# Splitting the accumulation step and shortening start-up in an attention and mixture-of-experts kernel on one core

## The chip, the cores and the metric

The kernel runs on one core of one Trainium2 chip. The metric is the device time of one launch in microseconds (us), lower is better; the time before is the median of three runs. The engines are TensorE (PE; its weight loads are listed as PEld), VectorE (DVE), ScalarE (ACT), GpSimd (POOL) and SyncE (SP, which here only issues DMAs). PSUM is the memory that TensorE writes; the others read it from there.

## The reference

Attention of 8 batches, 8 heads, 576 positions and 64 numbers a head, with a window of 32 positions and 8 global positions, whose result feeds a layer with 8 experts, of which each token takes the best one. In short:

```python
scores = scale * np.matmul(q, k.transpose(0, 1, 3, 2))
mask = np.abs(pos[:, None] - pos[None, :]) <= window
mask = mask | is_global[:, None] | is_global[None, :]
scores = np.where(mask, scores, -1000000000.0)
attn = softmax(scores)
attn_out = np.matmul(attn, v)
x = attn_out.transpose(0, 2, 1, 3).reshape(B * S, H * D)   # 4608 x 512
logits = x @ w_gate
expert_idx = np.argmax(logits, axis=1)
gate_w = softmax(logits)[np.arange(N), expert_idx]
for e in range(8):                       # 512 -> 1024 -> 512
    h = np.maximum(x[expert_idx == e] @ w1[e], 0.0)
    out[expert_idx == e] = gate_w * (h @ w2[e])
```

## The kernel before, in words

The order is written by hand: each engine has a queue in the order of the program, and an engine whose next instruction waits does nothing behind it. So the place of a line in the text is its place in the engine's queue.

**Start-up (to 28 us).** q, k and v of batch 0 are loaded (`load_qk` L158, `load_v` L163), q and k are cast to fp16 (`cast_qk` L289) and transposed on TensorE (`trans_qk` L293), masks are built, and twelve indirect DMAs on GpSimd (L264) gather the rows of the 8 global positions of all 8 batches from v, k and q. `trans_g` (L313) transposes the k and q rows, `load_vg` (L171) puts the v rows beside v.

**Attention (28 to 268.8 us), 8 batches of 6 slices t.** Loop L653 to L722. A slice: TensorE computes the scores of the next slice (`scores` L386: mask L392, products L405), ScalarE their exponentials (`exps` L410), TensorE the product with v of this slice (`pvs` L414, one PSUM buffer) and the sums (`zs` L428). Two accumulators, one half f each, collect the windows (`merge` L440): for half 0 ScalarE copies the new columns (L453) and VectorE adds the overlapping ones of half 1 (L458), then the same with the halves exchanged. Into slices 1 to 4 of all but the last batch go the transposes of the next batch's k and q (TensorE L300, L298; copied out of PSUM by ScalarE L305 for k, by VectorE L302 for q, the "q copy"). They share a PSUM pool of two buffers, `trp`, with everything below. The next batch's casts stand on GpSimd (L658).

The routing of the batch before (`class Tail`, L486) is spread over the same slices: `gate` L504, `logits` L518, `route1` L551 (arg-max), `ranks` L585 (place within the expert), `route2` L596 (slot), `rows` L539 (token rows transposed back into fp16), `scatter` L619 (six indirect DMAs on GpSimd, 128 token rows each). The weights of experts 0 and 1 are loaded in batches 1 to 4 in pieces of 512 KB (`wload` L633) and cast (`wcast` L640).

**Routing of the last batch (268.8 to 304 us).** L723 to L763: `sum_globals` and the memsets of eight row buffers (L725) on GpSimd, the routing of batch 7 and of the global rows (`tg`), the last scatters, then the first gathers of the experts' rows.

**Feed-forward stage (304 to 450 us).** Loop L935: for each expert eight h blocks of four matmuls (L943), each block through relu (L829, ScalarE and VectorE in turns), with a weight piece of an expert two ahead cast after every second block (`castp` L846) and its buffer loaded again (`fetch` L839). Then the four row tiles of the next expert are transposed (`xtrans` L809: four transposes, and a copy on VectorE L814), and four output blocks of eight matmuls follow (L969), scaled (L821, L823) and scattered. Blocks for overfull experts follow to 502 us and are not touched.

Of the kernel before, what the change touches and what calls it, by code (L numbers as in the profile page):

```python
# [22 lines left out]
NG = 8  # L23
# [20 lines left out]
def kernel(  # L44
# [42 lines left out]
    def short(*shape):  # L87
        n = 1
        for d_ in shape:
# [6 lines left out]
        r = stage[2 + a // 1024][:, a % 1024 : a % 1024 + n]  # L96
        return r.rearrange("p (a b) -> p a b", b=shape[1]) if len(shape) > 1 else r
# [64 lines left out]
    def load_v(b):  # L162
        d = vb[b % 2]  # L163
        for t in range(NT):
# [57 lines left out]
    nc.vector.scalar_tensor_tensor(out=p8s, in0=p8f, scalar=float(H * S), in1=rowb, op0=ALU.mult, op1=ALU.add)  # L222
    hofff = short(H)
# [17 lines left out]
    nc.vector.tensor_reduce(out=gip, in_=pmf, op=ALU.add, axis=AX.X)  # L241
    ridx = ap_.tile([128, H], I32, name="ridx")
# [70 lines left out]
    def trans_g():  # L313
        for src, dst in ((kg, kgt), (qg, qgt)):
# [4 lines left out]
            nc.vector.tensor_copy(dst, ps[:, 0:256].rearrange("p (c n) -> p c n", c=4))  # L319
# [21 lines left out]
    trans_g()  # L341
    fill_kg(0, nc.vector)
# [97 lines left out]
    def merge(t, parts):  # L440
# [11 lines left out]
        for i in range(len(parts)):  # L452
# [33 lines left out]
    class Tail:  # L486
# [64 lines left out]
        def route1(self):  # L551
# [12 lines left out]
            self.ex = small("ex", [6, 8])  # L564
            nc.scalar.activation(out=self.ex[p, 0:J], in_=d[p, 0:J], func=AF.Exp)
# [30 lines left out]
        def route2(self):  # L596
# [19 lines left out]
            nc.scalar.activation(out=self.x16[p, 0:J, DM:ROW].bitcast(I32)[:, :, 0],  # L616
                                 in_=tokg if self.glob else tokt[:, b, :], func=AF.Copy)
# [32 lines left out]
    routing_constants()  # L650
    tail = done = None
    staged = []
    for b in range(B):  # L653
# [8 lines left out]
        if b:  # L662
            sum_globals(b - 1)
# [418 lines left out]
```

## Time and profile before

| | |
|---|---|
| median of 3 runs | 504.03 us (503.88 to 504.34) |
| the profiled execution | 504.14 us, of which the profile's span is 502.4 us |
| mean granted TensorE clock | 0.93 |
| busy: PE, DVE, ACT, POOL | 76%, 49%, 40%, 49% |
| DMA traffic | 84.45 MB |

The span is the stretch that the profile covers, from its first to its last instruction; the rest of the execution's own time (1.74 us) lies around it. A busy share is an average over stages with different limits, so each stage is read by its own rows: an answer in order of time gives what an instruction waited for in brackets, with the idle time before it; "issue" there means that the profile shows nothing that it waited for.

### The profile page before, as it was taken

The numbers are of one execution on the slowest core, as the hardware profiler recorded it, in microseconds if no ns is written. First come the engines' busy times: TensorE is split into PE (matmuls) and PEld (weight loads), VectorE is DVE, ScalarE is ACT, GpSimd is POOL, SyncE is SP. The second block draws the span as 40 slices with busy tenths as digits, with TensorE's granted clock in tenths as the row PEclk, the third lists the DMA queues.
The fourth block names the chain that finished last, engine by engine and source line by source line (L and its number), as shares of the span: only waits on it lengthen the run. The fifth ranks groups of instructions, "written<-read, shape, count | busy, mean of one in ns | idle before, by whom it ended". The sixth has DMA issues, their size and how long they took to land. (4 is left out here: it accounts for less than half of the span.)

```text
span 502.4 us, 16112 instructions
## 1 busy us (share of the span) xinstructions
PE 383.6 (76%) x6595; PEld 233.1 (46%) x6595; DVE 248.3 (49%) x696; ACT 199.6 (40%) x359; POOL 246.5 (49%) x391
## 2 busy tenths in 40 slices
PE   1478686878877888889886509868888688999991
PEld 0256454556655665656563304434444243444540
DVE  3433253646665456666676704684455253233330
ACT  2235353654755547555440003325244233223330
POOL 6732350660836608475437765346466564334441
PEclk9999797989999799999998656999999989999996
DMA  7979989695897957721010274888999862112011
GB/s 166 190 177 170 214 189 274 144 283 139 195 284 155 274 132 179 165 35 51 8 46 14 74 253 139 284 311 264 341 332 327 310 190 102 66 64 71 31 42 38
DMA packets 76270, 84.45 MB, mean 168 GB/s; under 512 B 45084, under 2 KB 58412, under 8 KB 76192
## 3 DMA queue, kind: packets, MB, share of 16 engines
q1 hardware_dynamic: 66896, 63.61, 48.4%
q0 software_dynamic: 9024, 19.37, 11.6%
q8 instruction: 54, 0.88, 0.8%
q10 hardware_dynamic: 272, 0.39, 0.3%
q14 instruction: 24, 0.20, 0.1%
HBM read 68.89 MB, written 16.16 MB: 169 GB/s over the span
## 5 line engine op out<-in xcount | busy, mean ns | idle before, releaser
L943 PE MATMUL h<-xts,wall 128*128 128x512 f16 x256 | 62.0, 399 | 10.4 <-ACT ht L833 9.8
L423 PE MATMUL pv<-wall 56*64 56x128 f32 x1536 | 61.2, 294 | 6.5 <-issue 5.4
L458 DVE TENSOR_TENSOR xt<-xt,pv 128x288 f32<-128x288 f32 x80 | 36.3, 454 | 59.4 <-ACT xt L453 58.9
L412 ACT ACTIVATE wall<-sc 128x1024 f32<-128x1024 f32 x48 | 49.1, 1024 | 34.1 <-PE sc L405 32.5
L453 ACT ACTIVATE xt<-pv 128x224 f32<-128x224 f32 x96 | 34.3, 358 | 61.9 <-PE pv L423 29.9
L969 PE MATMUL yp<-wall,ht 128*128 128x512 f16 x256 | 56.6, 379 | 0.0
L423 PEld LDWEIGHTS pv<-wall 56*64 56x64 f32 x1536 | 47.0, 143 | 17.1 <-issue 13.3
L471 POOL TENSOR_TENSOR xt<-xt 128x144 f32<-128x144 f32 x14 | 7.1, 508 | 93.6 <-DVE xt L458 93.6
L287 POOL CAST wall<-wall 96x768 f16<-96x768 f32 (+1 forms) x56 | 43.9, 824 | 9.3 <-DMA wall<-in_k_dram 8.4
L943 PEld LDWEIGHTS <-wall 128*128 128x128 f16 x256 | 25.9, 102 | 45.1 <-issue 18.4
L824 POOL DMA_INDIRECT out_dram<-y,xr x24 | 25.0, 1041 | 41.4 <-DVE y L823 26.7
L831 DVE TENSOR_SCALAR ht<-h 128x512 f16<-128x512 f32 x32 | 22.1, 690 | 45.6 <-PE h L943 45.6
L435 PE MATMUL z<-wall,onesel 56*32 56x128 f32 x1536 | 36.7, 295 | 4.6 <-issue 4.6
L545 PE MATMUL tr_x<-id,xt 128*108 128x128 f32 x192 | 33.7, 303 | 6.9 <-DVE sv L602 2.2
L969 PEld LDWEIGHTS <-ht 128*128 128x128 f16 x256 | 24.7, 98 | 28.3
L833 ACT ACTIVATE ht<-h 128x512 f16<-128x512 f32 x32 | 19.0, 596 | 37.9 <-PE h L943 37.9
L405 PEld LDWEIGHTS <-kt 64*64 64x64 f16 x1536 | 25.1, 111 | 14.8 <-issue 10.1
L821 ACT ACTIVATE y<-yp,xr 128x512 f32<-128x512 f32 x12 | 8.2, 687 | 57.5 <-PE yp L969 37.1
L300 PE MATMUL tr_qk<-idh,wall 96*128 96x96 f16 x192 | 14.9, 219 | 19.7 <-ACT wall L285 11.0
L622 POOL DMA_INDIRECT xslot_scr<-wall,si x25 | 24.9, 995 | 8.7 <-issue 5.1
L785 POOL DMA_INDIRECT xr<-xslot_scr,idx x24 | 25.5, 1062 | 7.0 <-POOL xr L784 6.7
L622 POOL DMA_INDIRECT xslot_scr<-x16x,si x24 | 23.9, 994 | 9.0 <-issue 4.3
(243 smaller groups left out, 703.7 us busy)
## 6 DMA issues: line engine op xcount, KB each, us to landing
st<-in_moe_w_dram SPq DMA_DIRECT2D x48, 512.0 KB
wall<-in_k_dram SPq DMA_DIRECT2D x32, 288.0 KB
wall<-in_q_dram SPq DMA_DIRECT2D x32, 288.0 KB
wall<-in_v_dram SPq DMA_DIRECT2D x96, 96.0 KB
wall<-in_moe_w_dram SPq DMA_DIRECT2D x16, 512.0 KB
wall<-vg SPq DMA_DIRECT2D x16, 96.0 KB
xslot_scr<-wall,si POOLq DMA_INDIRECT x25, 2.6
wall<-in_q_dram ACTq DMA_DIRECT2D x1, 384.0 KB
```

Source lines behind the costliest of these rows:

```text
L287: eng.tensor_copy(o, i_)
L405: nc.tensor.matmul(out=o[:, NG:WE].rearrange("p (r a) -> p r a", r=R) if part == 0 else o[:, 0:NG], lhsT=kt[b % 2][rr, c, sl, :], rhs=rhs, ...
L412: nc.scalar.activation(out=e.rearrange("p r c w -> p r (c w)"), in_=sc[:, :, 0 : 4 * WE], func=AF.Exp, scale=0.125)
L423: nc.tensor.matmul(out=pv[64 * r : 64 * r + 64, f, c * WE : (c + 1) * WE], lhsT=vt[ff, t, 64 * h : 64 * h + 64], rhs=e[ff, r, c, :], start ...
L435: nc.tensor.matmul(out=z[32 * c : 32 * c + 32, f, 0:WE], lhsT=onesel[ff, r, :], rhs=e[ff, r, c, :], start=(r == 0), stop=(r == 1))
L453: nc.scalar.activation(out=new[i][0], in_=new[i][1], func=AF.Copy)
L458: nc.vector.tensor_tensor(out=d_, in0=d_, in1=s_, op=ALU.add)
L545: nc.tensor.transpose(out=ps[p, 128 * c : 128 * c + 128], in_=src, identity=id32)
L622: d_ = nc.gpsimd.indirect_dma_start(out=xslot, out_offset=IndirectOffsetOnAxis(ap=self.si[p, j : j + 1], axis=0), in_=self.x16[p, j, :].bi ...
L785: d_ = nc.gpsimd.indirect_dma_start(out=xr.bitcast(I16), out_offset=None, in_=xslot, in_offset=IndirectOffsetOnAxis(ap=ix, axis=0), bounds ...
L943: nc.tensor.matmul(out=ps, lhsT=w1v[:, e, c, 128 * fb : 128 * fb + 128], rhs=xts[:, c, :], start=(c == 0), stop=(c == 3))
L969: nc.tensor.matmul(out=ps, lhsT=ht[:, fc, 128 * j : 128 * j + 128], rhs=w2v[:, e, fc, :], start=(fc == 0), stop=(fc == 7))
```

## The change

It has five parts. In the words of the new code:

1. **Start-up.** Five small gathers (global rows of batch 0 only) stand before the scores, with a small `trans_g0`; the twelve large ones move behind `routing_constants`, and `trans_g`, with `load_vg(1)`, moves into slice 3 of batch 0. Only slice 0 of v is loaded ahead of them. 
2. **Batch 0.** The casts of batch 1 move from GpSimd to VectorE, one pair at the head of each slice 2 to 5, and the transposes of batch 1 from slices 1 to 4 to slices 2 to 5.
3. **The two halves.** `merge` returns a function for one half; the q transposes and the q copy (or `gate(0)`) stand between `mx(0)` and `mx(1)`.
4. **Routing.** `route2` moves ahead of the product of slice 5; its weights (`weights`), the exponentials and token numbers (`exps`) become steps of their own; `rows(2, 0)` moves from the next batch to the end of slice 5; the eight memsets move to the head of batch 7; after the loop the last scatters of batch 6 stand ahead of `sum_globals(7)`.
5. **Weights and feed-forward.** A weight piece is two DMAs of 128x512 instead of one; the rows of w1 in a DMA are 2 KB long instead of 4 KB. The four transposes of the next expert's rows stand one behind each second h block instead of all behind the last.

```diff
 def load_v(b, t0=None):
-    for t in range(NT):
+    for t in range(NT) if t0 is None else (t0,):
 load_qk(0)
+load_v(0, 0)
-load_v(0)
-for dst, src in ((vgr, v), (kg, k), (qg, q)):
-    for i in range(4):
-        ...
-for s_ in range(2):
-    nc.sync.dma_start(out=vg..., in_=vgr...)
+gather_g(vg0, v, ridx0[0:64, 2:3])
+for dst, src in ((kg0, k), (qg0, q)):
+    for r in range(2):
+        gather_g(dst[:, 64 * r : 64 * r + 64], src, ridx0[0:32, r : r + 1])
+for h in range(H):
+    nc.sync.dma_start(out=vg[0:8, h, :], in_=vg0[8 * h : 8 * h + 8])
 load_vg(0)
+for t in range(1, NT):
+    load_v(0, t)
...
+def trans_g0():
+    for i, src in enumerate((kg0, qg0)):
+        ps = trp.tile([128, 512], FP32, tag="tr", name="tr_g0")
+        nc.tensor.transpose(out=ps[:, 0:32], in_=src, identity=id32[0:32, 0:32])
+        p4 = ps[:, 0:32].rearrange("p (c o g) -> p c o g", c=4, o=1)
+        if i:
+            nc.vector.tensor_copy(qgt[:, :, 0:8], p4[:, :, 0])
+        else:
+            nc.vector.tensor_copy(kt[0][:, :, :, HW : HW + NG], p4.to_broadcast([128, 4, NSL, NG]))
 load_qk(1)
-trans_g()
-fill_kg(0, nc.vector)
+trans_g0()
...
 def merge(t, parts):
-    for i in range(len(parts)):
+    def part(i):
         nc.scalar.activation(out=new[i][0], in_=new[i][1], func=AF.Copy)
         ...
+    return part
...
 def wload(e, w, i, st):
-    if w == 0:
-        nc.sync.dma_start(out=st, in_=moe_w1[e, 128 * i : 128 * i + 128])
-    else:
-        ...
+    for hf in range(2):
+        src = (moe_w1[e, 128 * i : 128 * i + 128, 512 * hf : 512 * hf + 512] if w == 0
+               else moe_w2[e, 256 * i + 128 * hf : 256 * i + 128 * hf + 128])
+        nc.sync.dma_start(out=st[:, 512 * hf : 512 * hf + 512], in_=src)
...
 routing_constants()
+for dst, src in ((kg, k), (qg, q), (vgr, v)):
+    for i in range(4):
+        h = 4 * (i // 2) + i % 2
+        gather_g(dst[:, i, :], src, ridx[:, h : h + 1])
 for b in range(B):
-        for pair in range(4):
+        for pair in range(4) if b else ():
             cast_qk(pair, nc.gpsimd, nc.gpsimd)
...
     if b:
         sum_globals(b - 1)
+    if b + 1 == B:
+        for x_ in xr01:
+            nc.gpsimd.memset(x_, 0.0)
     for t in range(NT):
         tr = t - 1 if b + 1 < B and 1 <= t <= 4 else None
+        if b == 0:
+            tr = t - 2 if t >= 2 else None
+            if tr is not None:
+                cast_qk(tr, nc.vector, nc.vector)
         if tr is not None:
             trans_qk(b + 1, tr, "k")
+            if b == 0 and t == 5:
+                trans_qk(b + 1, tr, "q")
+                load_qk(2)
         elif t == 0 and done is not None:
-            done.rows(2, 0)
+            done.rows(2, 1)
+            done.scatter()
...
             elif t == 5:
                 tail.rows(1, 1)
+                tail.route2()
         pv = pvs(b, t)
-        merge_x(b, t, pv)
+        mx = merge_x(b, t, pv)
+        mx(0)
         if tr is not None:
-            trans_qk(b + 1, tr, "q")
+            if not (b == 0 and t == 5):
+                trans_qk(b + 1, tr, "q")
         elif t == 0 and tail is not None:
             tail.gate(0)
+        mx(1)
...
             elif t == 4:
                 tail.rows(1, 0)
+                tail.exps()
             else:
-                tail.route2()
+                tail.rows(2, 0)
+                tail.weights()
+        elif t == 3:
+            trans_g()
+            ...
+            load_vg(1)
+            fill_kg(1, nc.gpsimd)
+done.rows(2, 1)
+done.scatter()
 sum_globals(B - 1)
-for x_ in xr01:
-    nc.gpsimd.memset(x_, 0.0)
 tail.gate(0)
-done.rows(2, 0)
 tail.gate(1)
 tail.logits(0)
-done.rows(2, 1)
-done.scatter()
...
         if fb % 2:
             castp(nc.scalar if fb % 4 == 1 else nc.vector)
+            if e + 1 < E:
+                j = fb // 2
+                xtrans(rows_of[e + 1][j], xtn[:, :, 128 * j : 128 * j + 128])
     if e + 1 < E:
-        xts = fp2.tile([128, 4, 512], FP16, tag="xts", name="xts")
-        for j in range(4):
-            xtrans(rows_of[e + 1][j], xts[:, :, 128 * j : 128 * j + 128])
+        xts = xtn
```

How the instructions stand now is shown at three places. The first is VectorE's queue in a slice of batch 1 with transposes (`xt` and `zt` are the accumulators, `pv` and `z` the products in PSUM, `tr_qk` the transposes; the last three are `logits` of batch 0). Before:

```order
L458 TENSOR_TENSOR xt_76<-xt_76,pv 128x4x6x12 x2
L302 COPY qt_81<-tr_qk 128x6x96
L458 TENSOR_TENSOR zt_78<-zt_78,z 128x2x6x12
L529 RECIPROCAL rz<-tr_lt 108x16
L532 TENSOR_TENSOR tmp<-tr_lt,rz 108x128
L536 TENSOR_REDUCE lg<-tmp 108x16
```

and in the changed kernel, there as from batch 1 on:

```order
L479 TENSOR_TENSOR xt_76<-xt_76,pv 128x4x6x12
L310 COPY qt_81<-tr_qk 128x6x96
L479 TENSOR_TENSOR xt_76<-xt_76,pv 128x4x6x12
L479 TENSOR_TENSOR zt_78<-zt_78,z 128x2x6x12
L552 RECIPROCAL rz<-tr_lt 108x16
L555 TENSOR_TENSOR tmp<-tr_lt,rz 108x128
L559 TENSOR_REDUCE lg<-tmp 108x16
```

The q copy stands behind one add instead of two. The second place is VectorE's queue in batch 0, slices 2 and 3, of the changed kernel (`wall` are the buffers of k and q):

```order
L295 CAST wall<-wall 96x2x6x64
L295 CAST wall<-wall 128x2x6x64
L479 TENSOR_TENSOR xt_75<-xt_75,pv 128x4x6x12
L310 COPY qt_82<-tr_qk 128x6x96
L479 TENSOR_TENSOR xt_75<-xt_75,pv 128x4x6x12
L479 TENSOR_TENSOR zt_77<-zt_77,z 128x2x6x12
L295 CAST wall<-wall 96x2x6x64
L295 CAST wall<-wall 128x2x6x64
L479 TENSOR_TENSOR xt_75<-xt_75,pv 128x4x6x12
L310 COPY qt_82<-tr_qk 128x6x96
L479 TENSOR_TENSOR xt_75<-xt_75,pv 128x4x6x12
L479 TENSOR_TENSOR zt_77<-zt_77,z 128x2x6x12
```

Before, the two adds, the q copy and the add of `zt` stood there without casts; a slice's two casts now stand behind the last add of the slice ahead. The third place is VectorE's queue in an expert of the feed-forward stage (`ht` the blocks after relu, `st` a weight piece, `tx` the transposed rows). Before:

```order
L831 TENSOR_SCALAR ht<-h 128x512 x2
L645 CAST wall<-st 128x1024
L831 TENSOR_SCALAR ht<-h 128x512 x2
L645 CAST wall<-st 128x1024
L814 COPY xts<-tx 128x4x128 x4
L823 TENSOR_SCALAR y<-yp,xr 128x512
```

and now:

```order
L888 TENSOR_SCALAR ht<-h 128x512
L871 COPY xts<-tx 128x4x128
L888 TENSOR_SCALAR ht<-h 128x512
L674 CAST wall<-st 128x1024
L871 COPY xts<-tx 128x4x128
L888 TENSOR_SCALAR ht<-h 128x512
L871 COPY xts<-tx 128x4x128
L888 TENSOR_SCALAR ht<-h 128x512
L674 CAST wall<-st 128x1024
L871 COPY xts<-tx 128x4x128
L880 TENSOR_SCALAR y<-yp,xr 128x512
```

The four copies stood in a row ahead of the first output block, and stand now one behind each second block.

## Rows read from the trace of the kernel before

**Rows 1.** The page, its first line

```profile
span 502.4 us, 16112 instructions
```

**Rows 2.** Chronological answer, 0 to 45 us: start, duration (us), engine, line, operation

```profile
20.42 0.46 DVE L302 COPY qt<-tr_qk 128x576 f16<-128x576 f16 x1 [0.92 <-PE tr_qk L298]
...
25.29 1.62 SPq L174 DMA_DIRECT2D wall<-vg  x2
...
28.01 1.02 ACT L412 ACTIVATE wall<-sc 128x1024 f32<-128x1024 f32 x1 [8.40 <-PE sc L405]
...
31.77 1.98 PE L423 MATMUL pv<-wall 56*64 56x128 f32 x30 [1.01 <-DMA wall<-vg]
```

**Rows 3.** Chronological answer, batch 0: a score exponential and a value product

```profile
36.37 1.96 PE L423 MATMUL pv<-wall 56*64 56x128 f32 x32
36.66 1.02 ACT L412 ACTIVATE wall<-sc 128x1024 f32<-128x1024 f32 x1 [0.59 <-PE sc L405]
```

**Rows 4.** Chronological answer, the exponential that opens batch 1

```profile
53.40 1.02 ACT L412 ACTIVATE wall<-sc 128x1024 f32<-128x1024 f32 x1 [0.42 <-PE sc L405]
```

**Rows 5.** Groups by line: count, busy us, mean ns; then idle before and releasers

```profile
L287 DVE CAST wall<-wall 128x768 f16<-128x768 f32 x4 | 2.3, 579 | 3.6 <-DMA wall<-in_q_dram 3.6
```

**Rows 6.** TensorE's waits, 45 to 262 us: total us, times, longest

```profile
PE sc L405 <- issue: 8.2, 5, 4.3
PE tr_qk L300 <- DVE qt L302: 6.9, 9, 0.9
PE z L435 <- issue: 4.6, 3, 3.3
PE pv L423 <- issue: 4.2, 5, 1.8
PE tr_p L589 <- DVE qt L302: 3.7, 5, 1.0
PE tr_x L545 <- DVE sv L602: 2.2, 5, 0.5
```

**Rows 7.** Chronological answer, one slice of batch 5

```profile
196.03 0.45 DVE L458 TENSOR_TENSOR xt<-xt,pv 128x288 f32<-128x288 f32 x1 [1.17 <-ACT xt L453]
...
196.90 0.46 DVE L458 TENSOR_TENSOR xt<-xt,pv 128x288 f32<-128x288 f32 x1 [0.42 <-ACT xt L453]
...
197.28 0.45 DVE L302 COPY qt<-tr_qk 128x576 f16<-128x576 f16 x1
...
197.78 0.41 PE L300 MATMUL tr_qk<-idh,wall 96*128 96x96 f16 x6 [0.71 <-DVE qt L302]
...
199.13 1.10 PE L423 MATMUL pv<-wall 56*64 56x128 f32 x32
```

**Rows 8.** GpSimd in order of time, end of attention and routing

```profile
266.23 0.59 POOL L477 TENSOR_TENSOR gsum<-xt 128x192 f32<-128x192 f32 x1 [9.48 <-ACT xt L453]
...
269.11 3.82 POOL L725 MEMSET wall<- 128x516 f16 x8
273.11 1.00 POOL L622 DMA_INDIRECT xslot_scr<-wall,si  x1 [0.18 <-issue]
...
289.24 0.93 POOL L622 DMA_INDIRECT xslot_scr<-wall,si  x1 [0.30 <-issue]
```

**Rows 9.** Windows (busy us and count by engine, TensorE clock, DMA share, GB/s): batch 6, expert 4

```profile
216.74:244.44 27.70, 23.65 (x709) 17.09 (x709) 18.03 (x55) 14.16 (x30) 16.36 (x28) 1.00 0.16 33
...
376.90:394.10 17.20, 15.10 (x82) 7.20 (x80) 8.88 (x17) 7.32 (x10) 11.01 (x16) 1.00 0.96 339
```

**Rows 10.** TensorE's waits in the feed-forward stage, 304 to 450 us

```profile
PE tx L813 <- DVE xts L814: 10.1, 7, 3.1
PE h L943 <- ACT ht L833: 9.8, 7, 4.9
```

**Rows 11.** Windows while weight pieces stream during attention: w1, then w2

```profile
80.00:84.00 4.00, 1.26 (x14) 0.92 (x14) 0.16 (x1) 0.77 (x2) 0.00 (x0) 0.61 1.02 388
...
170.00:174.00 4.00, 3.78 (x72) 2.88 (x73) 2.15 (x7) 1.06 (x4) 3.05 (x4) 0.61 1.05 361
```

More of the change, by code (lines that the diff above doesn't have):

```diff
@@ L85, with short @@
     early = [0]
-    def short(*shape):
+    def short(*shape, parts=128):
         n = 1
-        for d_ in shape:
+        for d_ in shape if parts == 128 else shape[1:]:
             n *= d_
@@ L95, in short @@
         assert early[0] <= 2048
-        r = stage[2 + a // 1024][:, a % 1024 : a % 1024 + n]
-        return r.rearrange("p (a b) -> p a b", b=shape[1]) if len(shape) > 1 else r
+        r = stage[2 + a // 1024][0:parts, a % 1024 : a % 1024 + n]
+        return r.rearrange("p (a b) -> p a b", b=shape[1]) if len(shape) > 1 and parts == 128 else r
     x16b = [carve(TB, 6 * ROW, FP16).rearrange("p (j n) -> p j n", j=6)]
@@ L241 @@
     nc.vector.tensor_reduce(out=gip, in_=pmf, op=ALU.add, axis=AX.X)
+    ridx0 = ap_.tile([128, 3], I32, name="ridx0")
+    nc.vector.tensor_scalar(out=ridx0, in0=pre3, scalar1=gip, scalar2=None, op0=ALU.add)
     ridx = ap_.tile([128, H], I32, name="ridx")
@@ L340 @@
     load_qk(1)
-    trans_g()
-    fill_kg(0, nc.vector)
+    trans_g0()
+    for r in range(2):
+        nc.sync.dma_start(
+            out=wgbd[64 * r : 64 * r + 64, :, 8 * r : 8 * r + 8],
+            in_=moe_w_gate.rearrange("(c r p) e -> r p c e", c=4, r=2)[r])
     nc.vector.memset(qt[1][:, :, :, 0:6], 0.0)
@@ L458, in merge @@
                 nc.vector.tensor_tensor(out=d_, in0=d_, in1=s_, op=ALU.add)
+        return part
     def merge_x(b, t, pv):
-        merge(t, [(pv[:, f].rearrange("p (c w) -> p c w", c=4), xt[b % 2][:, f]) for f in range(2)])
+        return merge(t, [(pv[:, f].rearrange("p (c w) -> p c w", c=4), xt[b % 2][:, f]) for f in range(2)])
     def merge_z(b, t, z):
-        merge(t, [(z[:, :, 0:WE], zt[b % 2])])
+        merge(t, [(z[:, :, 0:WE], zt[b % 2])])(0)
     def join(b, eng):
@@ L583, in route1, with exps @@
                                         op=ALU.mult)
+        def exps(self):
+            p, J = slice(0, self.np), self.nj
+            self.ex = ap2.tile([TB, 6, 8], FP32, tag="ex", name="ex")
+            nc.scalar.activation(out=self.ex[p, 0:J], in_=self.d[p, 0:J], func=AF.Exp)
+            nc.scalar.activation(out=self.x16[p, 0:J, DM:ROW].bitcast(I32)[:, :, 0],
+                                 in_=tokg if self.glob else tokt[:, self.b, :], func=AF.Copy)
         def ranks(self):
@@ L611, in route2, with weights @@
                 nc.vector.tensor_tensor(out=self.si, in0=sl, in1=invbig, op=ALU.add)
+        def weights(self):
+            p, J = slice(0, self.np), self.nj
             sm = ap2.tile([TB, 6], FP32, tag="sm", name="sm")
@@ L677 @@
                 exps(n + 1, sc)
-            if t == 0 and done is not None:
-                done.rows(2, 1)
-                done.scatter()
-            elif tail is not None:
+            if tail is not None:
                 if t == 1:
@@ L722 @@
         tail = Tail(b)
+    tg = Tail(B)
+    done.rows(2, 1)
+    done.scatter()
     sum_globals(B - 1)
-    for x_ in xr01:
-        nc.gpsimd.memset(x_, 0.0)
-    tg = Tail(B)
     tail.gate(0)
-    done.rows(2, 0)
     tail.gate(1)
     tail.logits(0)
-    done.rows(2, 1)
-    done.scatter()
     tail.gate(2)
@@ L736 @@
     tail.route1()
+    tail.exps()
     tail.rows(0, 0)
@@ L739 @@
     tail.route2()
+    tail.weights()
     tail.rows(0, 1)
@@ L744 @@
     tg.route1()
+    tg.exps()
     tail.rows(1, 1)
@@ L747 @@
     tg.route2()
+    tg.weights()
     tail.rows(2, 0)
```

46 lines of the change are left out of this document (23 added, 23 removed).

## The prediction, made before the change was run

> **What bounds the kernel now.** I read the page first, then each stage by the view that shows its waits. The profiled execution took 504.14 us, 0.11 above the median of 504.03, with a span of 502.4 [rows 1]; the sum below is made against 504.14.
>
> *Start-up* I read in order of time [rows 2]. The last q copy of batch 0 begins at 20.42, but the first exponential only at 28.01 and the first product with v only at 31.77: the product waits for the global v rows (`vg`), whose load is issued at 25.29, behind the twelve gathers. So the end of start-up is set by GpSimd's gathers, not by the casts and transposes.
>
> *Attention* is bound by TensorE. In batch 6, with no weight loads, it is busy 23.65 of 27.70 us, VectorE 18.03, GpSimd 16.36 and ScalarE 14.16 [rows 9]. What is idle on TensorE shows in its waits from 45 to 262 us [rows 6]: for the q copy 6.9 (9 times, by k transposes, which need a `trp` buffer) and 3.7 (5 times, by `ranks`), for `sv` of `route2` 2.2, and 8.2 + 4.6 + 4.2 = 17.0 in 13 waits called "issue", behind which no instruction of another engine shows. In one slice of batch 5 the reader sees such a wait for the q copy: the two adds begin at 196.03 and 196.90, the copy behind them at 197.28, and the k transposes of the slice after waited 0.71 for it [rows 7].
>
> *Routing of the last batch* is a chain over VectorE, TensorE and GpSimd. On GpSimd the memsets begin at 269.11 and take 3.82 us; the scatters of batch 6 follow from 273.11 and the last of all begins at 289.24 [rows 8].
>
> *The feed-forward stage* is bound by TensorE with two kinds of waits: for the copies of the transposed rows 10.1 (7 times, longest 3.1) and for ScalarE's relu 9.8 [rows 10]. The DMA engines have no slack in expert 4: 0.96 busy at 339 GB/s [rows 9].
>
> **The change, part by part.**
>
> *Start-up: -5.0.* Five gathers in place of twelve stand ahead of the loads. Rows 8 give the step between two indirect DMAs on GpSimd: 13 of them (6 + 6 + 1) from 273.11 to 289.24, so at most 16.13 / 12 = 1.34 us each, with waits in it. Seven fewer are worth up to 9.4 us at GpSimd. The q copy at 20.42 then comes first: behind it stand `trans_g0`, two small copies and 32 score products. I put the first exponential at about 22.5 instead of 28.01, and the first product, which waits for `vg` no more, at 26.5 instead of 31.77: 5.0 to 5.5 earlier; I take 5.0. Bounds: nothing if the eight small loads of global v rows are late, and 7.5 if the first product comes right behind the exponential.
>
> *Batch 0: +4.2.* Between the exponentials at 36.66 and 53.40 lie four slices: 16.74 / 4 = 4.18 each [rows 3, 4]. In the changed order the VectorE of slices 2 to 5 runs two casts more, and the k transposes of TensorE wait for the first. A cast takes 0.579 us [rows 5], two 1.16. They stand behind the last add of the slice before, so that the chain add, q copy, add, add of `zt`, cast, k transposes can close on itself. I put a slice at 5.0: 4 x 0.82 = 3.3. The four transposes and two casts of `trans_g` come in too, about as long as a pair of k and q steps of one slice, TensorE's 0.41 and VectorE's 0.45 [rows 7]: +0.9. Bounds: zero if the casts fit into VectorE's idle time, 4 x 1.16 + 0.9 = 5.5 if all of it is waited for. So start-up and batch 0 together give -0.8.
>
> *The q copy between the halves: -7.5.* It comes behind one add rather than two, so it can begin at 196.90 - 0.42 = 196.48 in the slice of rows 7 rather than at 197.28: 0.80 earlier, against a wait of 0.71. The waits for it are 6.9 + 3.7 = 10.6 [rows 6]. I take 70%, since TensorE meets its next limit at some of them (the exponential, or the k copy). Behind the copy the second add is late by 0.45, and with it the free PSUM buffer of `pv`; the next product starts at 199.13 in rows 7, 2.2 us after the second add's beginning, which covers it. Bounds: 0 and -10.6.
>
> *Route2 earlier: -1.5* of the 2.2 that TensorE waits for `sv`; bounds 0 and -2.2. The exponentials and token numbers of the routing move on ScalarE, which is idle half of the time [rows 9]: nothing.
>
> *Routing of batch 7: -2.5.* The memsets (3.82) go to batch 7, where GpSimd, without casts for a batch 8, has room; the scatters of batch 6 can begin once the weights of slice 5 are there, at about 267 instead of 273.11. `sum_globals(7)` (from 266.23 to 269.11, 2.9 us) comes behind six of them: 267 + 6 x 1.3 + 2.9 = 277.7, before the scatters of batch 7, which now begin about 273.11 + 6 x 1.34 = 281. What is late next is the chain of token rows on TensorE and VectorE, which is shorter by `rows(2, 0)` and the eight small steps of `route2`, some 2.5 us. Bounds: 0 (that chain) and -3.8 (the memsets).
>
> *Feed-forward: -6.5* of the 10.1 [rows 10]. Each copy now has two h blocks to hide behind. Experts 0, 5 and 6, six of the seven waits being (10.1 - 3.1) / 6 = 1.17 each, return all: 3.5. The longest, 3.1, returns half, 1.5, since other VectorE work stands ahead of the copy. Experts 2 to 4 return 0.5 each: at 0.96 of the DMA engines 17.20 us can fall to 16.5 at the most [rows 9], and shorter rows cost part of that. Bounds: -3.5 and -10.1.
>
> *Weight pieces in halves: 0.* SP issues 64 more DMAs and is idle. In attention w1 streams with 4 KB rows at 388 GB/s and w2 with 2 KB rows at 361 [rows 11], both with the engines full, so half the bytes lose 7%: 3% on experts 2 to 4, counted above.
>
> Sum: -5.0 + 4.2 - 7.5 - 1.5 - 2.5 - 6.5 = -18.8, so **504.14 - 18.8 = 485.3 us**, 3.7% under the execution and the median alike.
>
> **The rivals.** About 0.2% (1 us) is what a measurement of this kernel can tell from no change.
>
> *The weight stream holds the experts.* Expert 4 stands at 0.96 of the DMA engines [rows 9]. If smaller pieces cost 7% on all of its stream, experts 2 to 4 grow by 3 x 17.2 x (0.07 x 0.96 - 0.04) = 1.4 instead of giving 1.5, and if experts 1 and 5, which share the stream, return nothing (2.7), the sum loses 5.6: 490.9. For it speaks the DMA row, against it that w2 already went in 2 KB rows. The Trainium skill, "DMA: Bandwidth & Descriptors", section "Rules for kernel authors", asks for 1 MiB or more in one DMA for the most bandwidth, which speaks against halving 512 KB. By the fit that the page gives, a fixed 2.0 us a DMA, the 48 pieces of the feed-forward stage would lose up to 96 us if the halves ran one behind the other, an estimate; rows 9 show 339 GB/s with several pieces under way at once, so the fixed part is already hidden, and the sum by the trace is the one that stands.
>
> *TensorE stays slow through batch 0.* The product of 32 matmuls took 1.96 us at 36.37 [rows 3] and 1.10 in batch 5 [rows 7]; TensorE had idled in start-up before the first. If the gaps that the casts leave keep it slow, a slice costs about 7.2 instead of 5.0 (0.86 more for this product, and as much again for sums, scores and transposes, 1.3): 4 x 2.2 = 8.8 more, 494.1.
>
> *The casts in batch 0 hide.* If the chain does not close, 4.0 of the 4.2 go: 481.3. For it speaks that VectorE had little in batch 0, two adds, a copy and an add a slice.
>
> *The q copy gives nothing.* If TensorE's own transposes of q, not the add ahead of the copy, are late, or if the waits only change their name: 7.5 back, 492.8. Against it: in rows 7 the copy begins right behind the add, with no wait for TensorE.
>
> *Slower: the "issue" waits grow.* 13 waits of 17.0, mean 1.31, longest 4.3 [rows 6], all behind work that the change reorders, in batches whose DMA engines it gives more and smaller transfers. At 3.0 each they come to 39.0, 22.0 more: 507.3. It decides from (17.0 + 18.8) / 13 = 2.75 a wait. For it speaks their size, against it that the bytes in flight stay the same. The Trainium skill, "Runtime: NRT & Kernel Launch", section "Instruction fetch mechanics", says that an engine fetches its next block of instructions by a DMA queue of its own while it runs, mostly hidden; if these waits are such fetches, rows 6 do not agree that they are hidden.
>
> **How the numbers follow.** Forecast 0.44; slow TensorE 0.17; casts that hide 0.13; weight stream 0.12; no gain from the q copy 0.08; issue waits 0.06. The predicted time is the likeliest, 485.3. Its own range, with the feed-forward bounds and the q copy's, is 481 to 490. The range of 8 in 10 takes in four of the rivals (481.3 to 494.1) and some of the bounds' ends beyond them: 477 to 496. Every case but the last is faster by well over 1 us: faster 0.92; of the last 0.06 most is slower, with what I have not seen 0.05; within 0.2% 0.03.
>
> **What would show it.** Right: first exponential near 22.5 and first product near 26.5; slices of batch 0 near 5.0; TensorE's waits for the q copy down to about 3; the last scatter about 2.5 nearer to the end of attention; its waits for the copied rows down to about 3.6, and expert 4 at 16.5 to 17.0 us. Wrong: a first product that waits for `vg` still, products of 1.96 us late in batch 0, "issue" waits above 17 in the same stretch, a DMA rate under 320 GB/s in experts 2 to 4.

## The result, and the profile after

The changed kernel took 483.29 us (median of 4 runs, 478.01 to 489.08), the kernel before 504.18 beside it: a ratio of 0.9544, 95% interval 0.9465 to 0.9624. The profiled execution took 483.26 us, its span is 481.5, 20.9 less than in [rows 1]. The changed kernel's runs lie 11 us apart, those of the kernel before 2. Both are more than the 1 us that the prediction took a measurement to tell, and it limits what single profiles can say of some stages below. Ratios are of mean times, without the runs that lie more than 1.5% above the fastest of their kernel, so they need not be those of the medians.

Where the 20.9 us are, by landmarks of the two traces (first exponential of a batch, first gather of the feed-forward stage, first h matmul):

| stretch | before | after | gain | forecast |
|---|---|---|---|---|
| to the first exponential | 28.01 | 23.21 | -4.8 | -5.0 |
| batch 0 | 25.39 | 33.60 | +8.2 | +4.2 |
| batch 1 | 35.99 | 29.51 | -6.5 | in the next row |
| batches 2 to 7, to the last exponential | 170.28 | 161.86 | -8.4 | -9.0, batch 1 with it |
| to the first gather | 32.96 | 32.18 | -0.8 | -2.5 |
| from there to the end | 209.8 | 201.1 | -8.6 | -6.5 |

The answer in order of time of the changed kernel, start-up and batch 0 (columns as in [rows 2]):

```profile
20.89 0.46 DVE L310 COPY qt<-tr_qk 128x576 f16<-128x576 f16 x1 [0.92 <-issue]
...
23.21 1.02 ACT L433 ACTIVATE wall<-sc 128x1024 f32<-128x1024 f32 x1 [3.16 <-PE sc L426]
...
27.64 1.98 PE L444 MATMUL pv<-wall 56*64 56x128 f32 x30 [1.21 <-DMA wall<-vg]
...
47.62 0.66 PE L308 MATMUL tr_qk<-idh,wall 96*128 96x96 f16 x6 [1.46 <-DVE wall L295]
...
49.27 1.95 PE L444 MATMUL pv<-wall 56*64 56x128 f32 x32
```

The last q copy of start-up is where it was (20.89, before 20.42), and the first exponential is 4.8 us earlier: start-up ends by the transposes now, with `vg` still a little late (1.21). In slice 4, k transposes wait for VectorE's cast, and the product behind them takes 1.95 again, as the early ones of the stage [rows 2, 3].

TensorE's waits in batch 0 (23 to 57 us), then in 45 to 262 us, as [rows 6]; the third fence has two lines of the kernel before that [rows 6] leaves out:

```profile
PE tr_qk L308 <- DVE wall L295: 5.9, 4, 2.0
PE pv L444 <- DMA wall<-vg: 1.5, 2, 1.2
```

```profile
PE sc L426 <- issue: 7.4, 4, 2.4
PE z L456 <- issue: 5.3, 3, 3.6
PE pv L444 <- issue: 4.6, 3, 2.3
PE sc L413 <- issue: 2.8, 1, 2.8
...
PE tr_qk L306 <- issue: 1.4, 1, 1.4
PE tr_qk L308 <- DVE qt L310: 1.0, 3, 0.5
```

```profile
PE tr_lt L524 <- issue: 1.8, 1, 1.8
...
PE tr_qk L298 <- issue: 1.0, 1, 1.0
```

The waits for the q copy went from 10.6 to 1.0, those for `sv` are gone. All "issue" waits together come to 21.5 in 12 waits, before to 19.8 in 15 (17.0 in [rows 6] and these two lines).

Windows of batches 0 and 1 before, and of batches 0, 1 and 6 and experts 2 to 5 after (columns as in [rows 9]):

```profile
28.01:53.40 25.39, 20.79 (x596) 15.52 (x599) 9.25 (x34) 13.20 (x25) 7.00 (x9) 1.00 0.95 198
53.40:89.39 35.99, 26.69 (x699) 18.84 (x688) 15.28 (x43) 14.32 (x29) 10.43 (x21) 0.81 0.94 221
```

```profile
23.21:56.81 33.60, 24.76 (x596) 18.74 (x599) 13.85 (x42) 13.41 (x25) 6.84 (x8) 0.81 0.77 156
56.81:86.32 29.51, 25.28 (x699) 18.56 (x692) 14.84 (x43) 14.31 (x30) 10.68 (x21) 0.87 0.93 202
...
208.07:231.51 23.44, 23.12 (x709) 17.01 (x708) 17.77 (x53) 14.30 (x32) 16.35 (x27) 1.00 0.22 45
...
325.98:341.70 15.72, 14.87 (x82) 7.16 (x81) 8.97 (x18) 7.32 (x10) 9.70 (x13) 1.00 0.99 349
341.70:357.44 15.74, 14.86 (x81) 7.16 (x80) 7.99 (x14) 7.32 (x10) 9.68 (x13) 1.00 1.03 373
357.44:373.72 16.28, 14.87 (x81) 7.12 (x80) 8.67 (x17) 7.32 (x10) 9.50 (x14) 1.00 0.99 349
373.72:397.49 23.77, 17.69 (x81) 8.05 (x80) 8.85 (x17) 7.32 (x10) 13.09 (x22) 0.86 0.61 216
```

Batch 0: TensorE is busy 4 us longer for the same 596 matmul records, at a granted clock of 0.81 where it had 1.00, and idle 4.2 longer (8.8 for 4.6). Batch 6: 23.12 of 23.44 us busy; it had been 23.65 of 27.70, so 3.7 of its 4.3 us are waits that are gone. Expert 4, 17.20 us before at 339 GB/s [rows 9], takes 16.28 at 349, expert 3 runs at 373.

TensorE's waits in the feed-forward stage after, which answer [rows 10]: no wait for the copied rows of the next expert is left, the one for ScalarE's relu has grown from 9.8.

```profile
PE h L1002 <- ACT ht L890: 12.5, 7, 6.1
```

GpSimd around the routing of batch 7, as [rows 8]:

```profile
258.30 0.99 POOL L652 DMA_INDIRECT xslot_scr<-wall,si  x1 [7.49 <-issue]
...
265.79 0.61 POOL L500 TENSOR_TENSOR gsum<-xt 128x192 f32<-128x192 f32 x1
...
269.31 1.00 POOL L652 DMA_INDIRECT xslot_scr<-x16x,si  x1 [0.67 <-DVE lsb L536]
...
277.08 0.94 POOL L652 DMA_INDIRECT xslot_scr<-wall,si  x1 [0.30 <-issue]
```

The first scatter starts 10.1 us after the last exponential (248.18), before it was 13.4 (259.67); then the sums of `sum_globals` (2.9 us, to 268.64) and a wait of 0.67 stand between two runs of scatters, 3.5 us in all, and the last scatter starts 28.9 us after that exponential, before 29.6.

### The profile page after: what moved, and what is told of

It is laid out like the page before. It is cut to its first block, busy times and chain, and to the rows that moved or that the text cites. A ratio compares the mean times of both kernels' runs of the same rounds, so it can differ in the third digit from the quotient of the medians.

```text
span 481.5 us, 16224 instructions
## 1 busy us (share of the span) xinstructions
PE 382.4 (79%) x6597; PEld 236.5 (49%) x6597; DVE 251.2 (52%) x709; ACT 198.9 (41%) x359; POOL 243.0 (50%) x388
## 5 line engine op out<-in xcount | busy, mean ns | idle before, releaser
L1002 PE MATMUL h<-xts,wall 128*128 128x512 f16 x256 | 65.8, 400 | 13.1 <-ACT ht L890 12.5
L444 PE MATMUL pv<-wall 56*64 56x128 f32 x1536 | 62.5, 301 | 6.1 <-issue 4.6
L444 PEld LDWEIGHTS pv<-wall 56*64 56x64 f32 x1536 | 49.0, 148 | 15.1 <-issue 11.6
L1002 PEld LDWEIGHTS <-wall 128*128 128x128 f16 x256 | 25.0, 101 | 42.1 <-issue 19.8
L456 PE MATMUL z<-wall,onesel 56*32 56x128 f32 x1536 | 35.5, 292 | 5.3 <-issue 5.3
L295 POOL CAST wall<-wall 96x768 f16<-96x768 f32 (+1 forms) x48 | 37.6, 822 | 2.0 <-DMA wall<-in_k_dram 1.6
L568 PE MATMUL tr_x<-id,xt 128*108 128x128 f32 x192 | 32.2, 302 | 4.1 <-DVE wall L569 1.7
L426 PEld LDWEIGHTS <-kt 64*64 64x64 f16 x1536 | 26.7, 116 | 13.7 <-issue 9.7
L652 POOL DMA_INDIRECT xslot_scr<-wall,si x25 | 24.9, 994 | 15.9 <-issue 13.0
L842 POOL DMA_INDIRECT xr<-xslot_scr,idx x24 | 26.7, 1112 | 6.9 <-POOL xr L841 6.9
L308 PE MATMUL tr_qk<-idh,wall 96*128 96x96 f16 x192 | 15.3, 222 | 18.6 <-ACT wall L293 11.2
L426 PE MATMUL sc<-qgt,kt 64*64 64x8 f16 x768 | 23.9, 173 | 6.0 <-issue 6.0
```

Of the source, the lines that this page charges most:

```text
L295: eng.tensor_copy(o, i_)
L426: nc.tensor.matmul(out=o[:, NG:WE].rearrange("p (r a) -> p r a", r=R) if part == 0 else o[:, 0:NG], lhsT=kt[b % 2][rr, c, sl, :], rhs=rhs, ...
L444: nc.tensor.matmul(out=pv[64 * r : 64 * r + 64, f, c * WE : (c + 1) * WE], lhsT=vt[ff, t, 64 * h : 64 * h + 64], rhs=e[ff, r, c, :], start ...
L456: nc.tensor.matmul(out=z[32 * c : 32 * c + 32, f, 0:WE], lhsT=onesel[ff, r, :], rhs=e[ff, r, c, :], start=(r == 0), stop=(r == 1))
L568: nc.tensor.transpose(out=ps[p, 128 * c : 128 * c + 128], in_=src, identity=id32)
L842: d_ = nc.gpsimd.indirect_dma_start(out=xr.bitcast(I16), out_offset=None, in_=xslot, in_offset=IndirectOffsetOnAxis(ap=ix, axis=0), bounds ...
```

## The experiments

Twelve runs in three groups, each group beside the kernel before on one chip. The third group (x10 to x13) fell on a chip on which the kernel before took 542.85 us; its kernels are compared with each other only. On the chips of the first two groups it took 504.33 and 504.51. All edits are to the changed kernel unless said otherwise.

**The chain through the casts.**

```diff
 if b == 0:
     tr = t - 2 if t >= 2 else None
-    if tr is not None:
-        cast_qk(tr, nc.vector, nc.vector)
+    for i_ in {2: (0, 1), 3: (2,), 4: (3,)}.get(t, ()):
+        cast_qk(i_, nc.vector, nc.vector)
```

> The changed kernel with each pair's casts of batch 0 one slice earlier in VectorE's queue (pairs 0 and 1 at slice 2, pair 2 at 3, pair 3 at 4). Theory: the chain that closes through the cast makes batch 0 long (k transposes waited 5.9 us for casts in 4 slices, batch 0 took 33.60). Then about 4 of the 5.9 go, batch 0 takes 28 to 30 us, and the time falls from 483.3 to about 479. Rival (TensorE's slow pace of slices 4 and 5 and the DMAs set it): batch 0 stays above 32 and the time within 1 us of 483.

483.19 us (481.06 to 486.73), ratio 0.9598 (0.9559 to 0.9638): no faster. Batch 0 fell by 4.0 to 29.57, as the theory had it, but batch 1 grew by the same 4.0 to 33.51:

```profile
22.54:52.11 29.57, 21.49 (x600) 16.14 (x603) 14.11 (x43) 12.79 (x25) 7.15 (x8) 0.88 0.84 176
52.11:85.62 33.51, 26.19 (x698) 18.41 (x690) 15.18 (x43) 14.27 (x31) 10.82 (x21) 0.85 0.88 200
```

Of the 4.0 us of batch 0, 3.3 are TensorE's busy time (24.76 to 21.49, at a granted clock of 0.88 for 0.81). Its idle time there fell by only 0.8, since another wait took the place of the casts': that of the products for `vg`, 7.0 us in 22 to 62 us, 4.0 of them in batch 1, where the changed kernel has 1.5 in all:

```profile
PE pv L444 <- DMA wall<-vg: 7.0, 4, 2.7
PE tr_qk L308 <- DVE wall L295: 3.4, 1, 3.4
```

```diff
-for pair in range(4) if b else ():
+for pair in range(4):
     cast_qk(pair, nc.gpsimd, nc.gpsimd)
...
-    if tr is not None:
-        cast_qk(tr, nc.vector, nc.vector)
```

> The changed kernel with the casts of batch 1 back on GpSimd, where they stand behind the twelve large gathers. Theory (cast chain): TensorE's waits for VectorE's cast go, and what is left is one wait of 3 to 6 us in slice 2, since the gathers end at about 31.4 us and eight casts of 0.82 take 6.6; batch 0 takes 29 to 31 us, time 479 to 481. Rival (the late data of q and k set it, not the engine that casts): the same 5 to 6 us are waited for casts on GpSimd, batch 0 stays above 32, time 483.

484.12 us (481.86 to 485.10). Batch 0 took 29.10 with one wait of 2.8 for GpSimd's cast, so the chain through VectorE's casts was the cause of its length, by its waits and by the slower TensorE that went with them (21.88 busy at 0.88); the waits for `vg` are 6.5 in 22 to 62 us, and batch 1 took 36.02. Which engine casts is not what decides the time.

**What is late next: the global v rows of batch 1.** In the changed kernel their two DMAs (L765) stand on SyncE behind twelve v loads (L167), and `load_vg(1)` (L174) behind both:

```profile
38.20 10.00 SPq L167 DMA_DIRECT2D wall<-in_v_dram  x12
48.38 1.83 SPq L765 DMA_DIRECT2D vg<-wall  x2
53.78 1.49 SPq L174 DMA_DIRECT2D wall<-vg  x2
```

```diff
-for dst, src in ((kg, k), (qg, q), (vgr, v)):
+for dst, src in ((vgr, v), (kg, k), (qg, q)):
...
+        if b == 0:
+            for s_ in range(2):
+                nc.sync.dma_start(out=vg..., in_=vgr...)
+            load_vg(1)
         load_v(b + 1)
```

> x1_cast_ahead, with the global v rows gathered first of the large gathers, and their placing for batch 1 ahead of the twelve v loads in SyncE's queue instead of behind them. Theory (what x1 gained in batch 0 was lost in batch 1 to the late vg, 7.0 us waited): that wait goes, batch 0 and 1 together take 59 us instead of 63.1, time about 479. Rival (the DMA engines, over 0.9 busy there, set it): the wait moves to v or to the casts' data, the two batches stay at 62 or more, time 482 to 483.

(The edit is made to x1_cast_ahead, and takes the two DMAs and `load_vg(1)` out of slice 3.) 482.10 us (479.60 to 483.61). Batches 0 and 1 together took 28.38 + 30.23 = 58.6 us, as the theory had it, 4.5 less than in x1. Batch 0 is idle for 9.15 us, not less than in the changed kernel (8.84); what it gained is TensorE's pace, at a granted clock of 1.00:

```profile
22.83:51.21 28.38, 19.23 (x600) 14.46 (x603) 13.78 (x42) 12.59 (x25) 6.86 (x8) 1.00 0.77 154
```

The time was 1.1 under x1's, less than the runs differ (the ratio 0.9536, 0.9496 to 0.9575, against 0.9598, 0.9559 to 0.9638). A new wait stood in batch 1, and batches 2 to 4 took 98.8 us, where the changed kernel had 95.1:

```profile
PE tr_qk L308 <- POOL wall L295: 5.8, 1, 5.8
```

k transposes of batch 2 now wait for GpSimd's casts. Batches 2 to 4 of x8 below, the same code there, took 93.0, so this stretch differs by almost 6 us from run to run and hides gains of this size.

**Are batches 2 to 4 held by the weights' bytes?**

```diff
-if t == 2:
+if t == 2 and b == 1:
     for p_, st_ in zip(staged, stage):
         wload(*p_, st_)
```

> The changed kernel with the weight pieces of batches 2 to 4 left out (12 of the 16 early pieces, 6.3 MB; the casts read the four pieces of batch 1 again, so experts 0 and 1 compute with other weights). Theory (batches 1 to 4 are held by the DMA engines, 230 GB/s at 0.94 busy, so that what start-up and batch 0 gain is given back there): batches 2 to 4, 29.3, 32.2 and 33.7 us, fall to 26 to 28 each, TensorE's issue waits there with them, time 12 to 18 less. Rival (TensorE's own work and its slow pace set these batches): they stay at 29 or more, time less than 5 down.

The kernel leaves out 12 of the 16 early pieces. 522.53 us (518.49 to 524.65), against 522.02 (518.36 to 528.10) of the changed kernel on that chip, for which the 481 to 485 of the other chips were expected:

> The changed kernel itself, for comparison on the same chip: 481 to 485.

Its windows of batches 2 to 4, without those pieces and (second fence) with them:

```profile
92.67:126.56 33.89, 30.19 (x709) 20.78 (x707) 17.91 (x53) 17.69 (x34) 16.41 (x27) 0.85 0.69 152
126.56:160.88 34.32, 29.68 (x710) 20.71 (x711) 17.95 (x54) 17.55 (x35) 16.34 (x27) 0.85 0.58 129
160.88:195.66 34.78, 28.33 (x709) 19.29 (x709) 17.93 (x53) 17.56 (x36) 16.33 (x27) 0.90 0.57 127
```

```profile
96.96:129.99 33.03, 29.24 (x709) 20.31 (x707) 17.91 (x53) 17.31 (x35) 16.40 (x27) 0.84 0.82 209
129.99:162.73 32.74, 27.70 (x710) 19.60 (x711) 17.94 (x54) 17.65 (x35) 16.32 (x27) 0.90 0.79 199
162.73:197.91 35.18, 29.52 (x709) 20.55 (x709) 17.82 (x53) 17.68 (x35) 16.33 (x27) 0.85 0.74 185
```

The DMA engines fall from about 0.8 to 0.6 busy, and the batches stay as long: 103.0 against 101.0 us. The theory that these bytes hold the stretch falls on this chip; on the first, where the DMA engines were 0.90 to 0.98 busy in these batches, it was not tried. "Issue" waits of 16.1 us in 26 pieces (batches 1 to 4) stayed, where the unedited kernel has 18.6 in 22.

**Start-up and batch 0 as before.** The edit puts back parts 1 and 2 of the change.

```diff
-gather_g(vg0, v, ridx0[0:64, 2:3])
-...
+for dst, src in ((vgr, v), (kg, k), (qg, q)):
+    for i in range(4):
+        ...
...
-if b == 0:
-    tr = t - 2 if t >= 2 else None
-    if tr is not None:
-        cast_qk(tr, nc.vector, nc.vector)
```

> The changed kernel with start-up and batch 0 as before (all twelve gathers ahead of the scores, casts of batch 1 on GpSimd, transposes in slices 1 to 4). Prediction's terms (-5.0 and +4.2): the time is 0.8 over the changed kernel's. Theory now (the DMA stretch of batches 1 to 4 takes back whatever the two give): within 1 of it. Rival (the first exponential 4.8 us earlier reaches the end): 3 to 5 over it. Second rival (batch 0's 8.2 more reach the end): 2 to 4 under it.

518.90 us (510.98 to 525.28), against 522.02 (518.36 to 528.10) with them: the ranges overlap, so no sign is settled, and none of the three expectations either. One thing on this chip speaks for the lower side. ScalarE began its first exponential at 27.84 in x12, but at 33.35 with the new start-up (33.51 and 33.32 in x10 and x11), though the scores were there as early as on the other chips (the last of their products ends at 22.95 in x13):

```profile
33.35 1.02 ACT L433 ACTIVATE wall<-sc 128x1024 f32<-128x1024 f32 x1 [13.20 <-remote]
```

So on this chip the new start-up was 5.5 us later, not 4.8 earlier. The profile names no instruction of this core for those 13.2 us ("remote"); no run here shows the cause.

**The q copy behind both halves again.**

```diff
 mx(0)
+mx(1)
 if tr is not None:
     ...
     trans_qk(b + 1, tr, "q")
-mx(1)
```

> The changed kernel with the q transposes and q copy (and the first gate) behind both halves of the accumulation, as before. Theory: the waits for the q copy return (10.6 us before, 1.5 now), batch 6 grows from 23.44 to about 25 and the time by 6 to 8 us to about 490. Rival (the earlier route2 and rows(2,0) made the gain of batches 5 to 7): the time grows by less than 2 us and batch 6 stays under 24.

489.91 us (487.56 to 493.22), ratio 0.9727 (0.9690 to 0.9765): 6.6 over the changed kernel's 483.29, and clear of it (the changed kernel's interval ends at 0.9624). Batch 6 and its waits:

```profile
211.30:237.75 26.45, 23.50 (x711) 17.24 (x710) 17.79 (x53) 14.32 (x30) 16.36 (x27) 1.00 0.20 41
```

```profile
PE tr_qk L308 <- DVE qt L310: 1.6, 2, 0.8
PE tr_p L618 <- DVE qt L310: 0.6, 1, 0.6
```

Of the 4.3 us that batch 6 gave, 3.0 come back with this edit alone; the other 1.3 belong to other parts, and no run divides them.

**Weight pieces whole.**

```diff
-for hf in range(2):
-    src = ...
-    nc.sync.dma_start(out=st[:, 512 * hf : 512 * hf + 512], in_=src)
+if w == 0:
+    nc.sync.dma_start(out=st, in_=moe_w1[e, 128 * i : 128 * i + 128])
+else: ...
```

> The changed kernel with each weight piece in one DMA again (512 KB; w1 in rows of 4 KB). Theory of the prediction (halves only cost some rate): experts 2 to 4, 15.72, 15.74 and 16.28 us now, fall by up to 0.5 each and the time by 0 to 1.5 us. Rival (the halves keep the stream moving, since a cast's buffer frees earlier and loads overlap): experts 2 to 4 go back towards 17.2 and the time grows by 2 to 4 us; TensorE's issue waits in batches 1 to 4 change with it.

483.05 us (479.47 to 489.44), ratio 0.9554 (0.9510 to 0.9597). Experts 2 to 4 took 15.26, 16.69 and 16.15, together 48.1 against 47.7 with halves, at 341 to 365 GB/s against 349 to 373; the issue waits of 45 to 250 us are 16.0, between those of x3 and x2 (14.7 and 19.8 in the same window). Halving the pieces is worth nothing that shows, either way.

**The row transposes behind the h blocks again.**

```diff
 if fb % 2:
     castp(...)
-    if e + 1 < E:
-        xtrans(rows_of[e + 1][j], xtn...)
...
+    for j in range(4):
+        xtrans(rows_of[e + 1][j], xts...)
```

> The changed kernel with the four row transposes of an expert behind its last h block again. Theory: the copies are waited for again (10.1 us over 7 experts before); experts 2 to 4 go from 15.7 to 16.3 us back to about 17.2 and the time grows by 6 to 9 us. Rival (the halved pieces made the experts shorter): experts 2 to 4 stay under 16.5 and the time grows by less than 3.

491.51 us (488.85 to 494.67), ratio 0.9725 (0.9678 to 0.9773): 8.2 over. The old wait is back in full:

```profile
PE tx L870 <- DVE xts L871: 10.3, 7, 3.3
PE h L1002 <- ACT ht L890: 7.1, 4, 4.7
```

Experts 2 to 4 went to 16.24, 16.25 and 16.94, expert 1 from 17.26 to 21.02. The theory holds for the sum, not for the places: it had 17.2 in experts 2 to 4. Experts 1 to 4 together took 70.5 us, 65.0 in the changed kernel and 71.2 before.

**GpSimd's order in the routing of batch 7.**

```diff
-    if b + 1 == B:
-        for x_ in xr01:
-            nc.gpsimd.memset(x_, 0.0)
...
-done.rows(2, 1)
-done.scatter()
 sum_globals(B - 1)
+for x_ in xr01:
+    nc.gpsimd.memset(x_, 0.0)
 tail.gate(0)
 tail.gate(1)
 tail.logits(0)
+done.rows(2, 1)
+done.scatter()
```

> The changed kernel with sum_globals and the eight memsets of 3.82 us ahead of the last scatters of batch 6 again. Theory (GpSimd's queue ends this stage): from the last exponential to the first gather 32.18 us becomes 34.5 to 36, time up 2.5 to 3.8. Rival (the chain of token rows on TensorE and VectorE ends it; before it took 32.96 from the last exponential, only 0.8 more): up by less than 1.

482.31 us (481.30 to 492.10), the same within what the runs differ. From the last exponential to the first gather it took 33.76, where the changed kernel has 32.18, and x5, x7 and x8, which have the changed kernel's order here and ran on the chip of x6, 32.65 to 32.94. So the order is worth about 1 us in this stretch, and nothing that shows in the time.

> x8_overflow_late with sum_globals of batch 7 ahead of the last scatters of batch 6, the memsets staying in batch 7. Theory (GpSimd's queue ends the routing of batch 7, and sum_globals, 3.5 us between two runs of scatters, took the place of the memsets): from the last exponential to the first gather 32.2 to 32.8 us becomes 29.5 to 30.5, time 2 to 3 under x8's 480.2. Rival (the chain of slots and token rows on VectorE and TensorE ends it): 32 to 33 as in the others, time within 1 of x8.

(On x8_overflow_late; only the line of `sum_globals` moves.) 519.91 us on the slower chip, ratio 0.9598, the changed kernel's there 0.9596, so on this chip x8's edits don't show either. The stretch took 33.87, not less than the changed kernel's 32.40 there (x13), so the theory is out; the rival's 32 to 33 was passed too. GpSimd, without the sums between, now waits in the second run of scatters:

```profile
302.83 0.99 POOL L652 DMA_INDIRECT xslot_scr<-x16x,si  x1 [2.19 <-DVE rz L552]
305.23 1.00 POOL L652 DMA_INDIRECT xslot_scr<-x16x,si  x1 [1.41 <-DVE sv L631]
```

So the rival's cause holds: the chain of slots and token rows on VectorE and the queue of 13 scatters end within some 2 us of each other (the last scatter begins 29.1 us after the last exponential in x13 and 30.6 here; on the chip of x6, 29.4 to 29.7 in x5, x7 and x8, and 30.5 in x6), and shortening one shows the other.

**A try at the largest stall left**, expert 5's 6.1 us. (The edit is made to x7_vg_first.)

```diff
-if e in (4, 5):
-    for i in range(3):
+if e == 6:
+    for i in range(6):
         ...
         gather(xr, ovi[...])
```

> x7_vg_first with the six gathers of overflow rows moved from experts 4 and 5 to expert 6, where GpSimd has no other gathers. Theory (GpSimd's queue of gathers and output scatters in experts 4 and 5 makes the stall of 5 to 6 us in expert 5): expert 5 falls from 21 to 24 us to 16 to 17, expert 6 grows by at most 2, time 4 to 6 under x7. Rival (the output rows' landing is late for another reason, the weight stream): expert 5 stays above 20.

480.24 us (477.20 to 482.18), ratio 0.9516 (0.9480 to 0.9553), x7's beside it 0.9536. Expert 5 fell from 22.86 (x7) to 16.11 us, as the theory had it, but the time by less than half of the 4 to 6 expected: expert 7 shows the wait next, 4.9 of these 7.4 us (from 352 us on). On GpSimd the six gathers now stand ahead of expert 6's output scatters, the first of which begins at 403.25, 0.30 after the last gather:

```profile
PE h L1003 <- ACT ht L891: 7.4, 3, 4.9
```

Its median is the lowest of this chip's group, 1.9 under x7's and 3 under the changed kernel's; the intervals overlap, so I don't call it faster than either.

## Why the prediction was right, and where it was not

The forecast was 485.3 us, the result 483.29: inside the range, and the sign and size were those of the likeliest case. The terms did not all hold, and three of the four signs of being wrong showed, each smaller than its rival needed: a first product 1.21 late for `vg`, a product of 1.95 us late in batch 0, and "issue" waits above 17. Only the DMA rate did not fall.

- **Start-up, -5.0: right** on the first exponential (-4.8). The first product gained 4.1 (31.77 to 27.64), less than the 5.3 put down, for `vg` was still 1.21 late. On the slower chip the exponential was later, not earlier (x12).
- **Batch 0, +4.2: mis-sized**, +8.2. The chain closed as described: k transposes waited 5.9 us for casts, where 4 x 0.82 = 3.3 stood in the sum; x1 and x2, which break it, take 4.0 and 4.5 off batch 0. The four slices took 24.9 us, 6.2 each, between the 5.0 of the sum and the 7.2 of the rival that TensorE stays slow. The step that failed is that the sum counted the chain as waits alone and put a slow TensorE into a rival of its own (0.17): about half of that rival came with the chain, TensorE being busy 4.0 us longer at a granted clock of 0.81, and this busy time is most of what x1, x2 and x7 win back.
- **What the sum left out: batch 1.** "So start-up and batch 0 together give -0.8" became +3.4, and batch 1, from which 1.7 us of waits for the q copy could go, gave 6.5: its "issue" waits fell from 7.6 (the two longest of [rows 6], 4.3 and 3.3) to 4.2 us and TensorE's busy time from 26.69 to 25.28. x1, x2 and x7 show why such a stretch can't be added term by term: they took 4.0 to 5.2 off batch 0 and were not clearly faster, since `vg`, then GpSimd's casts, were late next. The prediction had `load_vg(1)` only as something that moves along, and did not ask what stands ahead of it on SyncE's queue: twelve v loads, 10 us.
- **The q copy, -7.5: right.** Waits 10.6 to 1.0; putting it back costs 6.6 (x3), and its waits come back with it. The rival that it gives nothing is out.
- **Route2, -1.5: not shown.** The waits for `sv`, 2.2, are gone, but no run undoes this step alone. With the q copy put back (x3), batches 1 to 7 took 196.5 us, still 9.7 under the 206.3 before, where the sum had these 1.5. What gives the other 8 stays open: x4, with whole pieces, keeps them (188.4); parts 1 and 2 were undone on the slower chip only (x12, 229.9 for these batches, and 227.3 in x13 with them), part 4 by no run.
- **Routing of batch 7, -2.5: mis-sized**, -0.8. Even that is not clear of nothing: with the same order here the stretch took 32.2 to 33.4 in the traces of the changed kernel and x1 to x5, x7 and x8, and 32.96 before. The step that failed is that the chain of token rows, late next, "is shorter by `rows(2, 0)` and the eight small steps of `route2`, some 2.5 us". The scatters of batch 6 began 10.1 us after the last exponential where the forecast had 7.3 (267 against 259.67), and with the sums out of the way GpSimd waits for VectorE and is not done sooner (x10). The sums between the scatters fill its queue as the memsets did; x6 puts the order's worth at about 1 us in the stretch, and at nothing in the time.
- **Feed-forward, -6.5: mis-sized**, -8.6 to the end, 8.2 by x5. The step that failed is that experts 2 to 4 can't fall under 16.5 since the DMA engines are 0.96 busy: they fell to 15.7 to 16.3 at 349 to 373 GB/s and gave 4.1 where 1.5 stood. A busy share of 0.96 at 339 GB/s was not the stream's limit. Expert 5 gave nothing (22.90 before, 23.77 now): its wait for relu grew from 4.9 to 6.1 as that for the copies went, and TensorE was busy 0.9 longer (17.69 for 16.78).
- **Weight pieces, 0: right** (x4), and the rival of the weight stream is out. The Trainium skill, "DMA: Bandwidth & Descriptors", section "Anatomy of one DMA — SWDGE (gpsimd) path", fits about 2.0 us fixed to each DMA of GpSimd's path. The prediction's 96 us put that figure to pieces that SyncE issues, several under way at once, and no such cost shows there (x4: 48.1 us for experts 2 to 4 with whole pieces, 47.7 with halves).
- **Issue waits:** 17.0 in the sum, 19.8 with all groups before, 21.5 after; the slower case needed 35.8. They grew, as its sign said, but by far too little.

So the total came out within 2 us partly by luck, because errors met: start-up and batch 0 came out 4.2 dearer than put down and the routing 1.7, batches 1 to 7 5.9 cheaper (-14.9 where -9.0 stood) and the feed-forward stage 2.1.

## What to carry to other kernels

When the wait of a slot in a hand-written order disappears, look for what is issued behind the longest burst of loads on the same DMA-issuing queue: here that was late next (`vg`, behind twelve v loads), and three such edits (x1, x2, x7) were each right in their stage and worth nothing that the time shows. A copy that frees a two-buffer pool should stand behind as little as possible: moving it ahead of one 0.45 us add was worth 6.6 us over seven batches. A DMA busy share near 1 is not by itself a bound; see whether the consumer waits for a load. And read a gain in a stage by TensorE's busy and idle time apart: where x1 and x7 broke the chain of batch 0, most waits only changed their name, and what they gained was TensorE's pace.

## What the runs showed of the hardware

- TensorE's granted clock fell with gaps in its work. On the slower chip, batch 6 of the changed kernel (x13) has a stretch of a few matmuls at a time with "issue" waits of 0.3 to 0.5 us between them. In and behind it the clock goes from 1.00 (2.4 GHz) to 0.50 (1.2 GHz), where it stays while TensorE is busy again, and the last row has 0.99:

```profile
250.00:252.00 2.00, 1.23 (x8) 0.55 (x9) 0.51 (x1) 1.02 (x1) 1.68 (x2) 1.00 0.33 94
252.00:254.00 2.00, 0.86 (x6) 0.23 (x4) 0.18 (x1) 0.00 (x0) 0.99 (x1) 0.81 0.25 70
254.00:256.00 2.00, 1.69 (x38) 1.18 (x38) 1.02 (x3) 0.87 (x3) 0.00 (x0) 0.50 0.09 27
...
258.00:260.00 2.00, 2.00 (x34) 1.59 (x32) 0.69 (x1) 0.38 (x1) 0.00 (x0) 0.50 0.00 0
260.00:262.74 2.74, 2.60 (x89) 1.96 (x85) 2.06 (x5) 1.10 (x6) 0.00 (x0) 0.99 0.00 0
```

- Such waits can cost more than their own length: this batch took 31.96 us there and 23.44 on the first chip, 3.2 of the difference as idle time (3.56 for 0.32) and 5.3 as busy time (28.40 for 23.12, at a granted clock of 0.89 for 1.00). Expert 5 of the changed kernel is another case: after its wait of 6.1 TensorE is busy 17.69 us, at a granted clock of 0.86, where experts 2 to 4 have 14.87.
- A row's granted clock does not show all of TensorE's pace: batch 0 before has 1.00 in its row, though its early products took 1.98 and 1.96 us [rows 2, 3] and others 1.10 [rows 7].
- What causes the "issue" waits stays open; at a DMA share of 0.25 to 0.33, and with 6.3 MB of loads left out in x11, they were there all the same. The slower chip took 7.7% longer for the kernel before (542.85 against 504.18).
